# A fused attention and gated-MLP kernel: query weights built in wide pieces, early loads on two queues, a shorter inverse root, new load times

## The chip, the core and the metric

The kernel runs on one core of one Trainium2 chip. The core has a matrix engine (TensorE, in the profile PE, with its weight loads as PEld), a vector engine (VectorE, DVE), a scalar engine (ScalarE, ACT), GpSimd (POOL) and a sync engine (SyncE, SP) that issues DMAs; ACT and POOL can issue DMAs too. The metric is the device time of one execution in microseconds (us), and lower is better.

## The reference

All inputs are float32. Batch 8, 8 heads, 576 tokens, head size 64, 128 features.

```python
def phi(x):
    proj = np.einsum('bhsd,df->bhsf', x, w_phi)
    proj = proj - np.max(np.abs(proj), axis=-1, keepdims=True)
    return np.concatenate([np.exp(proj), np.exp(-proj)], axis=-1)
q_p, k_p = (phi(q), phi(k))
kv = np.einsum('bhsf,bhsd->bhfd', k_p, v)
z = np.sum(k_p, axis=2)
x = einsum(q_p, kv) / (einsum(q_p, z) + 1e-6)      # then heads side by side: (8, 576, 512)

h = np.maximum(x @ w_in, 0.0)                      # 512 -> 1024
u, v = h[..., :512], h[..., 512:]
v_n = (v - mean(v)) / np.sqrt(var(v) + 1e-06)
v_s = np.einsum('ts,bsd->btd', w_spatial, v_n) + b_spatial[None, :, None]
out = (u * v_s) @ w_out
```

## The kernel before

**Tiles.** The 576 tokens of a batch are 512 main tokens (four blocks of 128) and a tail of 64; the tails of two batches share one tile of 128 rows. The attention is worked in *units*, in a list written out at L567: a unit is a pair of heads of one batch (`pj` 0 to 3) over the main tokens, or the tail of a group of two batches. The list is: batch 0 pairs 0 and 1 (units 0, 1), the tail of group 0 (unit 2), pairs 2 and 3 (units 3, 4), batch 1 (units 5 to 8), the tail of group 1 (unit 9), batch 2 (units 10 to 13), batch 3, and so on to batch 7.

**A unit's path.** k and q are loaded as bfloat16 (`load`, L97, on POOL's DMA queue) and transposed: for batches 0 and 1 and for tails by PE through the identity (`a_transpose`, L249), for batches from 2 on by DMA transposes that SP issues three steps ahead (`cross`, L116, into `kT_b` and `qT_b`). `a_keys` (L271) multiplies by w_phi, takes the maxima on DVE (`mk`, L279) and the two exponentials on ACT (`kf`, L282). `a_scale` (L299) makes `em` on ACT (L302) and then multiplies v with it on POOL (`vs`, L307; for tails `tail_scale`, L317, into `vst`). `a_queries` takes the query maxima (`mq`, L293) and POOL splits them into two bfloat16 parts (`mhl`, L296 and L297); `a_max_t` (L326) transposes them on PE, and `a_qfeat` (L336) subtracts them within the matmul. From batch 2 on this uses the *query weights with maxima*, `wm`: eight blocks of 128 columns, the even ones holding the first half of w_phi with 16 rows of `sel` put below, the odd ones the second half with `sel` added (`weights_with_max`, L239). `q_even` (L245) copies a part of `qT_b` by DMA into `qt`. `a_kv` (L369), `a_num` and `a_x_t` follow, some steps later.

**The MLP.** When a batch's attention is done, `b_tasks` (L592) puts its MLP work into a queue, and `fill` (L620) hands out tasks from that queue between the attention's parts, by credit. Per batch: `b_v` (matmul on PE at L448, Relu on ACT at L450, statistics on DVE at L451 and L452), `b_root` (the inverse root of the variance on POOL, `root`, L454), `b_ln` (normalization on POOL, `normalize`, L464, one instruction of 128x512 per block, L465), `b_u` (L503), `b_s` (the spatial matmul, L524, which reads the normalized tiles `vn`) and `b_o` (L549). The spatial weights are loaded for batch 0 as `wsp`, `wspr` and `wspt` and transposed on PE into `w_spT` (`transpose_spatial`, L210); the bias goes into one row of `w_spT` for each of the two tails by four ACT copies at the end of that function. `vnt` holds the normalized tails; its other rows are filled once with a column of the identity so that the bias row counts.

**What sets the order.** The main loop (L713) runs `step(i)` for each unit and then the DMA work that the table `io` holds for that step. `pin` keeps an instruction in the order of the program on its engine. Each engine and each DMA queue runs its instructions in order, so on POOL a DMA issue stands in line with the scalings, and on SP a transpose that waits for a load holds up what is queued behind it. The start (L123 to L190) loads w_phi on ACT; k and q of heads 0 to 3, the k and q tails (into a staging tile `tails`), v and the v tail on SP in this order. DVE casts heads 0 and 1, POOL heads 2 and 3 and the tails. The other half of the heads is loaded by POOL in quarters (L185 to L190).

In the table of step numbers before the change, batch 2's k and q loads are issued at steps 4, 4, 6 and 7, the spatial weights at 4 and 5, the second part of w_in at 6, w_out at 8.

Of the kernel before, what the change touches and what calls it, by code (L numbers as in the profile page):

```python
# [16 lines left out]
def kernel(  # L17
# [105 lines left out]
    wphi_f = cpool.tile([P, F], FP32)  # L123
    for i in range(2):
        nc.scalar.dma_start(out=wphi_f[i * D:(i + 1) * D, :], in_=w_phi)
    alloc(0)
    first = {}
    for h0 in (0, 2):
        for x, t in (("k", k), ("q", q)):
            first[x, h0] = s2.tile([P, 2, NB * D], FP32, tag="ob", name="first", bufs=6)  # L130
            pin(nc.sync.dma_start)(out=first[x, h0], in_=main_ap(t, 0, h0, 2))
    alloc_tail(0)
    tails = ld.tile([P, H * NB, D], FP32, tag="v_f", name="tails")
    for n, t in enumerate((k, q)):
        for i in range(2):
            pin(nc.sync.dma_start)(out=tails[i * TL:(i + 1) * TL, n * H:(n + 1) * H, :], in_=tail_ap(t, i))
    load_v(0, 0)
    load_tail("v", 0)
    load_v(0, 1)
    ident = cpool.tile([P, P], BF16)  # L140
    make_identity(nc, ident)
    zero = cpool.tile([P, 1], BF16)
    pin(nc.vector.memset)(zero, 0.0)
# [25 lines left out]
    pin(nc.vector.memset)(vst[1], 0.0)  # L169
# [7 lines left out]
    pin(nc.scalar.copy)(out=vst[0].rearrange("p b s h d -> p (b s h d)"), in_=zero.to_broadcast([P, 4 * H * DA]))  # L177
# [3 lines left out]
    for i in range(2):  # L181
        fill_vnt(i, nc.gpsimd.tensor_copy)
    for x in ("k", "q"):
        pin(nc.gpsimd.tensor_copy)(out=half_tile(x, 0, 0)[:, 2:4], in_=first[x, 2])
    load("k", 0, 1, 0, 2)  # L185
    load("q", 0, 1, 0, 2)
    for n, x in enumerate(("k", "q")):
        pin(nc.gpsimd.tensor_copy)(out=gs[0][x], in_=tails[:, n * H:(n + 1) * H, :])
    load("k", 0, 1, 2, 2)
# [4 lines left out]
    wsp = s2.tile([P, NB, T0], BF16, tag="vn", name="wsp", bufs=2)  # L194
    wspr = cpool.tile([P, NB, TL], BF16)
    wspt = s2.tile([TL, S], BF16, tag="ob", name="wspt", bufs=6)
    bsp_row = s2.tile([P, S], FP32, tag="xT", name="bsp_row", bufs=3)
    nc.sync.dma_start(out=bsp_row[TL:TL + 1, :], in_=moe_b_spatial)
    nc.sync.dma_start(out=bsp_row[0:1, :], in_=moe_b_spatial)
# [10 lines left out]
    def transpose_spatial(i):  # L210

        pt = psum.tile([P, S], BF16, tag="bank", name="pt")
        if i < NB:
            sc = POS[i]
            for tp, c in enumerate(POS):
                nc.tensor.transpose(out=pt[:, tp * P:(tp + 1) * P], in_=wsp[:, c, bass.ds(sc, P, step=NB)],
                                    identity=ident)
            nc.tensor.transpose(out=pt[:, T0:S], in_=wspt[:, bass.ds(sc, P, step=NB)],
                                identity=ident[:TL, :TL])
            nc.vector.tensor_copy(out=w_spT[:, i, :], in_=pt)  # L220
            return
        for bl in range(2):
            lo = bl * TL
            for tp, c in enumerate(POS):
                nc.tensor.transpose(out=pt[lo:lo + TL, tp * P:(tp + 1) * P], in_=wspr[:, c, :], identity=ident)
            nc.tensor.transpose(out=pt[lo:lo + TL, T0:S], in_=wspt[:, T0:S], identity=ident[:TL, :TL])
            nc.vector.tensor_copy(out=w_spT[lo:lo + TL, NB + bl, :], in_=pt[lo:lo + TL, :])
        for bl, row in ((0, TL), (1, 0)):
            r = slice(row, row + 1)
            pin(nc.scalar.copy)(  # L230
                out=w_spT[r, NB + bl, 0:T0].rearrange("o (a b p) -> o a b p", a=2, b=2),
                in_=bsp_row[r, 0:T0].rearrange("o (p b a) -> o a b p", a=2, b=2))
            pin(nc.scalar.copy)(out=w_spT[r, NB + bl, T0:S], in_=bsp_row[r, T0:S])
# [4 lines left out]

    def weights_with_max(n):  # L239
        for j in range(4 * n, 4 * n + 4, 2):  # L240
            pin(nc.gpsimd.tensor_copy)(out=wm[:, j, :], in_=wphi2[:, 0:F])
            pin(nc.gpsimd.tensor_tensor)(out=wm[:, j + 1, :], in0=wphi2[:, F:2 * F], in1=sel[:, j + 1, :], op=ALU.add)
            pin(nc.gpsimd.tensor_copy)(out=wm[D:D + 2 * H, j, :], in_=sel[0:2 * H, j, :])
# [210 lines left out]
    def root(mv, r, n):  # L454

        var = small.tile([P, NB, 1], FP32, tag="var", name="var")
        rs = small.tile([P, NB, 2], FP32, tag="rs", name="rs")
        nc.gpsimd.tensor_scalar(out=var[r, 0:n], in0=mv[r, 0:n, 1:2], scalar1=1e-6, scalar2=None, op0=ALU.add)
        nc.gpsimd.tensor_tensor(out=rs[r, 0:n, 0:1], in0=var[r, 0:n], in1=neghalf[r, 0:n].unsqueeze(2), op=ALU.pow)
        nc.gpsimd.tensor_tensor(out=var[r, 0:n], in0=mv[r, 0:n, 0:1], in1=rs[r, 0:n, 0:1], op=ALU.mult)  # L460
        nc.gpsimd.tensor_scalar(out=rs[r, 0:n, 1:2], in0=var[r, 0:n], scalar1=-1.0, scalar2=None, op0=ALU.mult)
        return rs

    def normalize(dst, src, rs):  # L464
        nc.gpsimd.tensor_scalar(out=dst, in0=src, scalar1=rs[:, 0:1], scalar2=rs[:, 1:2],  # L465
                                op0=ALU.mult, op1=ALU.add)

    def b_v(b, j):
        d = st[b]
        if j == 0:  # L470
            d["vn"] = s2.tile([P, NB, HALF], BF16, tag="vn", name="vn", bufs=2)
            d["mv"] = small.tile([P, NB, 2], FP32, tag="mv", name="mv")
            d["vr"] = {}
        d["vr"][j] = s2.tile([P, HALF], BF16, tag="vr", name="vr", bufs=5)
        stats = small.tile([P, 6], FP32, tag="stats", name="stats")
        v_mm(lambda kc: d["xT"][:, kc, j * P:(j + 1) * P], d["vr"][j], slice(0, P), stats, d["mv"][:, j, :])

    def b_root(b):
        st[b]["rs"] = root(st[b]["mv"], slice(0, P), NB)

    def b_ln(b, j):
        d = st[b]
        normalize(d["vn"][:, j, :], d["vr"][j], d["rs"][:, j, :])

    def b_v_tail(g, bls):
# [6 lines left out]
        rstd = root(mv, r, 1)  # L492
        for bl in bls:
            r = slice(bl * TL, (bl + 1) * TL)
            normalize(vnt[g % 2][r, bl, :], vr[r], rstd[r, 0, :])
# [96 lines left out]
    def b_tasks(b):  # L592
# [8 lines left out]
        ts.append((0.0, lambda: b_root(b)))  # L601
# [79 lines left out]
    at(1, load_v, 1)  # L681
    at(2, load, "k", 1, 0)
    at(2, load, "q", 1, 0)
    at(3, load, "k", 1, 1)
    at(3, load, "q", 1, 1)
    at(4, load_weight, w_in_bf[:, :, HALF:DFF], cols[:, :, HALF:DFF])
    at(4, load_weight, wspt, moe_w_spatial[T0:S, :])
    at(5, tail_scale, 0, 1)
    at(5, load_weight, wsp, rows[:, :, 0:T0])
    at(5, load_weight, wspr, rows[:, :, T0:S])  # L690
    at(6, load_weight, w_in_bf[:, :, 0:HALF], cols[:, :, 0:HALF])
    at(8, load_weight, w_out_bf, moe_w_out.rearrange("(kc p) f -> p kc f", p=P))
    for u in units:
        i = u["i"]
        if not u["pair"] and u["g"] > 0:
            early = 1 if u["g"] > 1 else 0
            at(i - AT - early, load_tail, "k", u["g"])
            for x in ("q", "v"):
                at(i - AT + 1 - early, load_tail, x, u["g"])
        if u["pair"] and u["b"] >= XB:  # L700
            if u["pj"] == 0:
                for n, (x, y) in enumerate((("k", 0), ("q", 0), ("k", 1), ("q", 1))):
                    at((4, 4, 6, 7)[n] if u["b"] == XB else i - AB + n, load, x, u["b"], y)
# [4 lines left out]
    at(6, weights_with_max, 0)  # L708
    at(7, weights_with_max, 1)
# [39 lines left out]
```

## Time and profile before

Eight runs, device time in us; one execution was profiled.

| what | value |
|---|---|
| median of 8 runs | 284.66 us |
| lowest, highest | 282.31, 286.45 us |
| the profiled execution | 285.06 us, of which the trace's span is 283.0 us |
| PE busy | 259.7 us (92%), 3042 matmuls |
| DVE busy | 231.2 us (82%) |
| ACT busy | 219.6 us (78%) |
| POOL busy | 200.5 us (71%) |
| DMA | 42.43 MB, mean 150 GB/s |

The page gives a digit for each of 40 equal slices of the span (7.1 us each), tenths of the slice in which the engine was busy. A table of stages gives the same in microseconds for stretches that one chooses. The chain of waits is followed back from the last instruction: at each step to what released it. The timeline lists instructions in order of time, and in brackets the idle time before one and what ended it. A busy PE is not a PE at its peak, since its ends are modelled.

### The profile page before, as it was taken

The numbers are of one execution on the slowest core, as the hardware profiler recorded it, in microseconds if no ns is written. First come the engines' busy times: TensorE is split into PE (matmuls) and PEld (weight loads), VectorE is DVE, ScalarE is ACT, GpSimd is POOL, SyncE is SP. The second block draws the span as 40 slices with busy tenths as digits, with TensorE's granted clock in tenths as the row PEclk, the third lists the DMA queues.
The fourth block names the chain that finished last, engine by engine and source line by source line (L and its number), as shares of the span: only waits on it lengthen the run. The fifth ranks groups of instructions, "written<-read, shape, count | busy, mean of one in ns | idle before, by whom it ended". The sixth has DMA issues, their size and how long they took to land.

```text
span 283.0 us, 8175 instructions
## 1 busy us (share of the span) xinstructions
PE 259.7 (92%) x3042; PEld 172.9 (61%) x3042; DVE 231.2 (82%) x576; ACT 219.6 (78%) x499; POOL 200.5 (71%) x362
## 2 busy tenths in 40 slices
PE   2777988987999999999999999999999999999993
PEld 1466865754766577666666775666666765654441
DVE  7969997875799988998889989997889897566341
ACT  5679996979399997899889987899789977723601
POOL 5997999999958886799949974889548832411710
PEclk9979999999799999999999999999999999999999
DMA  7998999999977999989989999999765301120305
GB/s 203 227 216 111 157 141 228 126 175 185 215 78 164 145 216 188 165 185 225 231 101 122 205 251 147 204 199 225 92 122 132 86 2 63 50 76 37 112 3 185
DMA packets 85148, 42.43 MB, mean 150 GB/s; under 512 B 52146, under 2 KB 80498, under 8 KB 85108
## 3 DMA queue, kind: packets, MB, share of 16 engines
q1 hardware_dynamic: 60020, 30.95, 55.1%
q0 software_dynamic: 24928, 10.89, 35.6%
q8 instruction: 24, 0.39, 0.6%
q14 instruction: 16, 0.13, 0.2%
q10 hardware_dynamic: 160, 0.07, 0.1%
HBM read 32.85 MB, written 9.44 MB: 149 GB/s over the span
## 4 chain that ended last, share of the span: by engine, by line
PE 63%; POOL 12%; ACT 9%; DVE 6%; DMA 4%; issue 3%; SPq 0%; POOLq 0%; ACTq 0%; DVEq 0%
PE ps L524 10%; PE pv L448 10%; PE po L549 9%; PE ps L267 7%; PE pu L503 6%; ACT kf L282 5%; PE pv L379 4%; PE pn L399 4%; PE pq L345 3%; PE ps L525 3%; DMA q_bf<-in_q_dram 2%; POOL vst L61 2%; POOL vs L307 2%; DVE stats L451 2%; DMA first<-in_q_dram 2%
## 5 line engine op out<-in xcount | busy, mean ns | idle before, releaser
L282 ACT ACTIVATE kf<-ps 128x512 bf16<-128x512 f32 x144 | 76.1, 634 | 9.9 <-DVE mk L279 9.5
L307 POOL TENSOR_TENSOR vs<-v_f,em 128x512 bf16<-128x512 f32 x64 | 65.5, 1044 | 18.9 <-ACT em L302 17.5
L366 ACT ACTIVATE qf<-pq 128x512 bf16<-128x512 f32 x128 | 66.6, 618 | 10.1 <-PE pq L345 8.5
L279 DVE TENSOR_REDUCE mk<-ps 128x4 f32<-128x512 f32 x72 | 47.6, 677 | 1.2 <-PE ps L267 0.5
L293 DVE TENSOR_REDUCE mq<-ps 128x4 f32<-128x512 f32 x62 | 39.8, 681 | 2.7 <-PE ps L267 1.4
L524 PE MATMUL ps<-w_spT,vn 128*128 128x512 bf16 x128 | 34.1, 382 | 2.7 <-POOL vn L465 2.7
L527 DVE TENSOR_TENSOR uT<-ps,uT 128x512 bf16<-128x512 f32 x32 | 22.0, 687 | 16.7 <-PE ps L525 16.7
L451 DVE BATCH_NORM_STATS2 stats<-vr 128x6 f32<-128x512 bf16 (+1 forms) x40 | 26.7, 684 | 7.3 <-ACT vr L450 6.9
L549 PE MATMUL po<-w_out_bf,uT 128*128 128x512 bf16 x128 | 32.3, 379 | 0.0
L503 PE MATMUL pu<-xT,w_in_bf 128*128 128x512 bf16 x128 | 32.1, 379 | 0.0
L448 PE MATMUL pv<-w_in_bf,xT 128*128 128x512 bf16 x128 | 31.5, 379 | 0.1
L450 ACT ACTIVATE vr<-pv 128x512 bf16<-128x512 f32 (+1 forms) x40 | 23.5, 614 | 7.6 <-PE pv L448 6.4
L379 PE MATMUL pv<-vs,kf 128*128 128x66 bf16 x512 | 24.3, 193 | 1.3 <-ACT kf L282 1.3
L390 DVE TENSOR_TENSOR x<-pn,rc 128x256 bf16<-128x256 f32 x64 | 24.9, 417 | 0.3
L465 POOL TENSOR_SCALAR vn<-vr,rs 128x512 bf16<-128x512 bf16 x32 | 24.3, 766 | 1.1
L399 PEld LDWEIGHTS <-qf 128*128 128x128 bf16 x512 | 20.5, 98 | 7.1 <-issue 1.4
L505 ACT ACTIVATE uT<-pu 128x512 bf16<-128x512 f32 x32 | 19.6, 638 | 4.9 <-PE pu L503 3.2
L379 PEld LDWEIGHTS <-kf 128*128 128x128 bf16 x512 | 21.8, 97 | 2.5 <-issue 1.5
L552 ACT COPY ob<-po 128x512 f32<-128x512 f32 x18 | 11.0, 612 | 14.9 <-PE po L549 8.4
L399 PE MATMUL pn<-kv,qf 128*128 128x66 bf16 x512 | 22.0, 195 | 0.3 <-ACT qf L366 0.3
L381 PE MATMUL pv<-vst,kf 128*128 128x66 bf16 x128 | 21.2, 191 | 0.0
L524 PEld LDWEIGHTS <-vn 128*128 128x128 bf16 x128 | 11.7, 98 | 13.7 <-POOL vn L465 4.4
(133 smaller groups left out, 572.5 us busy)
## 6 DMA issues: line engine op xcount, KB each, us to landing
out_dram<-ob SPq DMA_DIRECT2D x32, 256.0 KB, 2.9
v_f<-in_v_dram SPq DMA_DIRECT2D x14, 512.0 KB, 6.6
k_bf<-in_k_dram POOLq DMA_DIRECT2D x14, 256.0 KB, 6.3
q_bf<-in_q_dram POOLq DMA_DIRECT2D x14, 256.0 KB, 6.7
qt<-qT_b SPq DMA_DIRECT2D x24, 64.0 KB, 4.8
v_tl<-in_v_dram SPq DMA_DIRECT2D x8, 128.0 KB, 3.5
v_f<-in_v_dram SPq DMA_DIRECT2D x1, 1024.0 KB, 9.3
w_in_bf<-in_moe_w_in_dram POOLq DMA_DIRECT2D x2, 512.0 KB, 9.6
```

What stands on the lines that cost most here:

```text
L279: nc.vector.tensor_reduce(out=u["mk"][:, hs], in_=pk, axis=AX.X, op=ALU.max, apply_absolute_value=True)
L282: nc.scalar.activation(out=u["kf"][:, s, hs, :], in_=pk, func=AF.Exp, bias=0.0, scale=sc)
L293: nc.vector.tensor_reduce(out=mq[:, 4 * half:4 * half + 4], in_=pq, axis=AX.X, op=ALU.max, apply_absolute_value=True)
L307: nc.gpsimd.tensor_tensor(out=vs[:, s, :, 0:D], in0=st[u["b"]]["v"][:, pj * H:(pj + 1) * H, :], in1=em[:, s, :].unsqueeze(2).to_broadcast( ...
L366: nc.scalar.activation(out=qf[:, s], in_=pq, func=AF.Exp, bias=0.0, scale=sc)
L379: nc.tensor.matmul(out=pv[:, hh, s, :], lhsT=u["kf"][:, s, 4 * hh + c, :], rhs=u["vs"][:, s, 4 * hh + c, :], start=(c == 0), stop=False)
L399: nc.tensor.matmul(out=pn[:, pos, :], lhsT=u["qf"][hh][:, s, pos, :], rhs=d["kv"][:, 2 * u["pj"] + hh, s, :], start=(s == 0), stop=(s == 1))
L448: nc.tensor.matmul(out=pv[r], lhsT=lhs(kc), rhs=w_in_bf[:, kc, HALF:DFF], start=(kc == 0), stop=(kc == KC - 1))
L451: nc.vector.bn_stats(out=stats[r], in_=dst[r])
L503: nc.tensor.matmul(out=pu, lhsT=w_in_bf[:, kc, dc * P:(dc + 1) * P], rhs=d["xT"][:, kc, :], start=(kc == 0), stop=(kc == KC - 1))
L524: nc.tensor.matmul(out=ps, lhsT=d["vn"][:, sp, cs], rhs=w_spT[:, sp, 0:T0], start=(sp == 0), stop=False)
L549: nc.tensor.matmul(out=po[r], lhsT=lhs(dc), rhs=w_out_bf[:, dc, :], start=(dc == 0), stop=(dc == KC - 1))
```

## The change

In words, part by part:

- **Start.** w_phi is issued first, on ACT; after it ACT also issues q of heads 2 and 3 and the q tails. SP issues k and q of heads 0 and 1, k of heads 2 and 3, the k tails, then the first half of v and the v tail. The tails are staged in the second half of batch 0's v tile instead of a tile of their own, so the second half of v is loaded after POOL has cast them. POOL casts k of heads 2 and 3, issues a quarter of k, casts q, issues a quarter of q.
- **Bias.** The bias rows are loaded by POOL right at the start, and POOL copies them into `w_spT` there; the four ACT copies at the end of `transpose_spatial` go.
- **Fills.** `vst[0]` is cleared by POOL as float32 words instead of an ACT copy of zeros; `vst[1]` by DVE as before. `vnt[1]` is filled at step 11 instead of at the start.
- **Query weights.** The even blocks of `wm` are written by two wide ACT copies at the start, the odd ones by one wide POOL addition at step 3, instead of twelve narrow POOL instructions at steps 6 and 7.
- **Spatial weights.** `wspr` goes; `wsp` holds all 576 columns and is loaded by one DMA at step 4. `wspt` moves to step 6.
- **Load times.** The second part of w_in moves from step 6 to 5, w_out from 8 to 9, batch 2's k and q from 4, 4, 6, 7 to 7, 7, 8, 9, its v to 8 and 9, batch 3's k and q by one step. The tail loads of group 1 are at steps 5 and 6.
- **Root.** The addition of the epsilon and the negated mean are made by DVE right after the statistics (`moments`), so the root on POOL is two instructions instead of four. For tails the root and the normalization become tasks of their own, behind the v matmuls.
- **Normalization.** For the last batch it runs on DVE.

```diff
+    tails = st[0]["v"][:, 2 * H:4 * H, :]
+    def load_first(x, h0, eng):
+        first[x, h0] = s2.tile([P, 2, NB * D], FP32, tag="ob", name="first", bufs=6)
+        pin(eng.dma_start)(out=first[x, h0], in_=main_ap(k if x == "k" else q, 0, h0, 2))
-        nc.scalar.dma_start(out=wphi_f[i * D:(i + 1) * D, :], in_=w_phi)
-    for h0 in (0, 2):
-        for x, t in (("k", k), ("q", q)):
-            first[x, h0] = s2.tile([P, 2, NB * D], FP32, tag="ob", name="first", bufs=6)
-            pin(nc.sync.dma_start)(out=first[x, h0], in_=main_ap(t, 0, h0, 2))
-    tails = ld.tile([P, H * NB, D], FP32, tag="v_f", name="tails")
-    for n, t in enumerate((k, q)):
+        pin(nc.scalar.dma_start)(out=wphi_f[i * D:(i + 1) * D, :], in_=w_phi)
+    load_first("k", 0, nc.sync)
+    load_first("q", 0, nc.sync)
+    load_first("q", 2, nc.scalar)
+    load_first("k", 2, nc.sync)
+    for n, t, eng in ((1, q, nc.scalar), (0, k, nc.sync)):
         for i in range(2):
-            pin(nc.sync.dma_start)(out=tails[i * TL:(i + 1) * TL, n * H:(n + 1) * H, :], in_=tail_ap(t, i))
+            pin(eng.dma_start)(out=tails[i * TL:(i + 1) * TL, n * H:(n + 1) * H, :], in_=tail_ap(t, i))
     load_v(0, 0)
     load_tail("v", 0)
-    load_v(0, 1)
...
-    pin(nc.vector.memset)(vst[1], 0.0)
+    bsp_row = s2.tile([P, S], FP32, tag="xT", name="bsp_row", bufs=3)
+    for r in (TL, 0):
+        pin(nc.gpsimd.dma_start)(out=bsp_row[r:r + 1, :], in_=moe_b_spatial)
+    for i, eng in ((0, nc.gpsimd), (1, nc.vector)):
+        pin(eng.memset)(vst[i].rearrange("p b s h d -> p (b s h d)").bitcast(FP32), 0.0)
...
-    pin(nc.scalar.copy)(out=vst[0].rearrange("p b s h d -> p (b s h d)"), in_=zero.to_broadcast([P, 4 * H * DA]))
-    for i in range(2):
-        fill_vnt(i, nc.gpsimd.tensor_copy)
+    fill_vnt(0, nc.gpsimd.tensor_copy)
+    for bl, r in ((0, TL), (1, 0)):
+        row, bias = w_spT[r:r + 1, NB + bl, :], bsp_row[r:r + 1, :]
+        pin(nc.gpsimd.tensor_copy)(out=row[:, 0:T0].rearrange("o (a b p) -> o a b p", a=2, b=2),
+                                   in_=bias[:, 0:T0].rearrange("o (p b a) -> o a b p", a=2, b=2))
+        pin(nc.gpsimd.tensor_copy)(out=row[:, T0:S], in_=bias[:, T0:S])
+    def alternate(t, i):
+        return t.rearrange("p (j two) f -> p j two f", two=2)[:, :, i, :]
+    pin(nc.scalar.copy)(out=alternate(wm, 0), in_=wphi2[:, 0:F].unsqueeze(1).to_broadcast([P, NP, F]))
+    pin(nc.scalar.copy)(out=alternate(wm[D:D + 2 * H], 0), in_=alternate(sel[0:2 * H], 0))
+    def odd_weights():
+        pin(nc.gpsimd.tensor_tensor)(out=alternate(wm, 1), in0=alternate(sel, 1),
+                                     in1=wphi2[:, F:2 * F].unsqueeze(1).to_broadcast([P, NP, F]), op=ALU.add)
     for x in ("k", "q"):
         pin(nc.gpsimd.tensor_copy)(out=half_tile(x, 0, 0)[:, 2:4], in_=first[x, 2])
-    load("k", 0, 1, 0, 2)
-    load("q", 0, 1, 0, 2)
+        load(x, 0, 1, 0, 2)
     for n, x in enumerate(("k", "q")):
         pin(nc.gpsimd.tensor_copy)(out=gs[0][x], in_=tails[:, n * H:(n + 1) * H, :])
+    load_v(0, 1)
...
-        nc.gpsimd.tensor_scalar(out=var[r, 0:n], in0=mv[r, 0:n, 1:2], scalar1=1e-6, scalar2=None, op0=ALU.add)
-        nc.gpsimd.tensor_tensor(out=rs[r, 0:n, 0:1], in0=var[r, 0:n], in1=neghalf[r, 0:n].unsqueeze(2), op=ALU.pow)
-        nc.gpsimd.tensor_tensor(out=var[r, 0:n], in0=mv[r, 0:n, 0:1], in1=rs[r, 0:n, 0:1], op=ALU.mult)
-        nc.gpsimd.tensor_scalar(out=rs[r, 0:n, 1:2], in0=var[r, 0:n], scalar1=-1.0, scalar2=None, op0=ALU.mult)
+    def moments(mv, r, n):
+        m = small.tile([P, NB, 2], FP32, tag="var", name="var")
+        nc.vector.tensor_scalar(out=m[r, 0:n, 0:1], in0=mv[r, 0:n, 1:2], scalar1=1e-6, scalar2=None, op0=ALU.add)
+        nc.vector.tensor_scalar(out=m[r, 0:n, 1:2], in0=mv[r, 0:n, 0:1], scalar1=-1.0, scalar2=None, op0=ALU.mult)
+        return m
+    def root(m, r, n):
+        nc.gpsimd.tensor_tensor(out=rs[r, 0:n, 0:1], in0=m[r, 0:n, 0:1], in1=neghalf[r, 0:n].unsqueeze(2), op=ALU.pow)
+        nc.gpsimd.tensor_tensor(out=rs[r, 0:n, 1:2], in0=m[r, 0:n, 1:2], in1=rs[r, 0:n, 0:1], op=ALU.mult)
+    def normalize(b, dst, src, rs):
+        eng = nc.vector if b == B - 1 else nc.gpsimd
+        eng.tensor_scalar(out=dst, in0=src, scalar1=rs[:, 0:1], scalar2=rs[:, 1:2], op0=ALU.mult, op1=ALU.add)
...
+    at(11, fill_vnt, 1, nc.gpsimd.tensor_copy)
+    at(3, odd_weights)
-    at(4, load_weight, wspt, moe_w_spatial[T0:S, :])
+    at(4, load_weight, wsp, rows)
-    at(5, load_weight, wsp, rows[:, :, 0:T0])
-    at(5, load_weight, wspr, rows[:, :, T0:S])
-    at(6, load_weight, w_in_bf[:, :, 0:HALF], cols[:, :, 0:HALF])
-    at(8, load_weight, w_out_bf, moe_w_out.rearrange("(kc p) f -> p kc f", p=P))
+    at(5, load_weight, w_in_bf[:, :, 0:HALF], cols[:, :, 0:HALF])
+    at(5, load_tail, "k", 1)
+    at(6, load_tail, "v", 1)
+    at(6, load_tail, "q", 1)
+    at(6, load_weight, wspt, moe_w_spatial[T0:S, :])
+    at(7, load, "k", 2, 0)
+    at(7, load, "q", 2, 0)
+    at(8, load, "k", 2, 1)
+    at(8, load_v, 2, 0)
+    at(9, load, "q", 2, 1)
+    at(9, load_v, 2, 1)
+    at(9, load_weight, w_out_bf, moe_w_out.rearrange("(kc p) f -> p kc f", p=P))
-                    at((4, 4, 6, 7)[n] if u["b"] == XB else i - AB + n, load, x, u["b"], y)
+                    at(i - AB + n + (u["b"] == 3), load, x, u["b"], y)
-    at(6, weights_with_max, 0)
-    at(7, weights_with_max, 1)
```

## The prediction

> **What bounds the kernel now.** I read the busy shares in slices first, then a table of 10 us stages, then the chain of waits where TensorE (PE) is not full, then single waits, last the landing times of the DMAs. From the slices:
>
> ```profile
> PE   2777988987999999999999999999999999999993
> DVE  7969997875799988998889989997889897566341
> POOL 5997999999958886799949974889548832411710
> ```
>
> PE falls short in the first ten slices (7.1 us each) and at the end. The stages give sizes (stretch, length, busy us of PE, PEld, DVE, ACT, POOL, then clock, DMA share, GB/s):
>
> ```profile
> 10.00:20.00 10.00, 6.66 (x57) 4.78 (x58) 7.61 (x22) 6.57 (x16) 9.98 (x16) 0.83 1.05 242
> 20.00:30.00 10.00, 8.22 (x159) 7.39 (x155) 10.00 (x29) 9.40 (x23) 7.97 (x12) 1.00 0.85 108
> ...
> 50.00:60.00 10.00, 8.87 (x109) 6.51 (x105) 7.80 (x22) 9.91 (x21) 9.17 (x21) 1.00 1.44 149
> 60.00:70.00 10.00, 8.38 (x103) 5.57 (x101) 6.85 (x15) 8.55 (x22) 9.30 (x17) 1.00 1.36 175
> ```
>
> PE idles 283.0 - 259.7 = 23.3 us: 8.9 before 20 (5.1 of it before its first transpose), 2.6 in 20 to 40, 4.8 in 40 to 80, 1.7 in 80 to 260, 5.2 after that (4.5 of it from 270 on, the drain of the last outputs). The edit leaves PE's instructions and their order as they are, so what can be won is idle time. From 19.4 to 42 VectorE (DVE) is full, so nothing on GpSimd (POOL) is worth anything there. The chain of waits, in pieces (start, us, what):
>
> ```profile
> 9.45 6.92 DMA q_bf<-in_q_dram
> ...
> 35.52 2.25 POOL vst L61 x3
> 37.77 0.68 POOL wsp L61
> 38.46 0.73 POOL wspr L61
> 39.19 1.39 POOL q_tl L61 x2
> ```
>
> A query load ends the wait at 16.4. From 29.4 to 43.3, and again from 54.0 to 70.7, the chain is POOL without a break: scalings, DMA issues, roots. The single waits (timeline, in brackets the idle time before the instruction) show where PE pays:
>
> ```profile
> 43.29 0.23 PE L328 MATMUL pt<-ident,mhl 128*128 128x128 bf16 x1 [1.56 <-POOL mhl L297]
> ...
> 59.07 0.38 PE L267 MATMUL ps<-wphi,kT_b 128*128 128x256 bf16 x2 [1.13 <-ACT qf L366]
> ...
> 69.22 0.39 PE L524 MATMUL ps<-w_spT,vn 128*128 128x512 bf16 x1 [1.25 <-POOL vn L465]
> 69.97 0.39 PE L524 MATMUL ps<-w_spT,vn 128*128 128x512 bf16 x1 [0.36 <-POOL vn L465]
> 70.72 0.61 PE L524 MATMUL ps<-w_spT,vn 128*128 128x512 bf16 x1 [0.36 <-POOL vn L465]
> ```
>
> The transfers are uneven. These are medians from issue to landing, the first for 18 to 34 us, the other two for 36 to 60:
>
> ```profile
> k_bf<-in_k_dram POOLq DMA_DIRECT2D x3, 256.0 KB, 4.3
> ...
> k_bf<-in_k_dram POOLq DMA_DIRECT2D x2, 256.0 KB, 12.7
> ...
> kT_b<-k_bf SPq DMA_TRANSPOSE x3, 11.0
> ```
>
> **What the Trainium skill says.** "DMA: Bandwidth & Descriptors", section "Issuing engines are not separate DMA queues": a second issuing engine saves only issue time, the 16 DMA engines are shared. The slow landings above, with transposes in flight, agree. So "two queues" is worth issue time, no bandwidth. Its section "SWDGE vs HWDGE vs iDMA": a load that casts must be issued by GpSimd; k, q and the weights do cast, so their issues (0.7 to 0.8 us each) stay on POOL. "GPSIMD Engine Reference", section 3.1: about 1.8 cycles an element for one input (768 ns for 512) and 2.6 for two; the trace has 767 ns (L465) and 1044 ns (L307). "VectorE: DVE Perf Modes", section "The perf-mode tier table": `tensor_scalar` from bf16 in SBUF runs four elements a cycle; no row of before has that form.
>
> **The change part by part.**
>
> *Start.* k and q of heads 0 and 1 keep their place on SP; q of heads 2 and 3 and the query tails go behind w_phi on ScalarE (ACT). ACT issues three more DMAs (0.5 + 2 x 0.7) before its table load, but loses the 1.95 us fill of vst: its w_phi casts end near 1.9 + 1.9 + 1.3 + 0.6 = 5.7, as before (5.71). POOL gains two bias issues (nearest rows 0.56 to 0.8 each), a 1056-word fill (DVE's took 0.94) and four bias copies (ACT's took 2.52 together; a POOL cast of 512 elements 0.61, so 1.6 to 3.2), and loses two of four vnt copies (1.37). It reaches its first k cast at 1.36 + 1.3 + 0.95 + 1.37 + 1.6 to 3.2 = 6.6 to 8.2, against 6.84 when the data came. The q load of the next half follows a k cast, a k issue and a q cast (0.6 + 0.8 + 0.6): issue at 8.9 to 10.3, against 9.45. In return the second half of v waits for the tails staged in it (POOL's q_tl cast, near 11 instead of an issue at 8.88), and batch 1's v queues behind it. Without that 0.5 MB and with no bias rows on SP, the load should land nearer 4.8 than 6.9 us after issue: near 14.8 instead of 16.4. DVE's idle around it (0.86 + 1.32 + 0.21 = 2.4 us) is the most to win; 2.3 us of PE work stands between the landing and DVE's mT copy, which leaves about 1.3. Late bias rows could make it -1.0. I take **-1.3** (range -2.4 to +1.0).
>
> *POOL from 28.6 to 56.2.* It is busy 25.0 of the 27.6 us up to the end of unit 8's scaling, counted instruction by instruction. Twelve wm pieces (4 x 0.30 + 4 x 0.43 + 4 x 0.28 = 4.0) become one two-input row of 512 elements (1.05, at step 3, behind unit 3's scaling) and two ACT copies at the start. One spatial issue goes (0.74); one q load of batch 2 and w_out (1.6) move behind the first normalization. I count 18.9 us in the new order, 6 us less. It buys only what PE idles. (a) Unit 6's maxima reach PE by 38, so the waits at 43.29 and 44.40 (1.56 + 0.17) go: **-1.4**, since DVE, full until 42, is next. (b) The bias copies leave ACT at 55.5 (2.52 us ahead of the qf that PE waited on at 59.07): **-0.9** of 1.13. (c) The root is two POOL instructions shorter (0.24 + 0.25, twice), and with the 6 us the normalized tiles come near 63, before PE asks: **-1.6** of 1.97. If ACT or DVE, 99% and 78% busy at 50 to 60, end these waits instead, (a) to (c) fall to about -1.5 together.
>
> *Loads of batch 2.* Both loads of its first half are issued from POOL near 42 and 45 instead of 31.3 and 32.0; SP's transposes, queued in order, wait for them. PE wants the first kT near 57.6 - 2.6 = 55. At 4.3 us for a load in a window now free of transposes and 5.3 for a transpose (its median at 56 to 92) it lands at 51.6; qT near 55.5 with 57 wanted. Margins of 2 to 3 us, so a small charge: **+0.7**, range 0 to +10 (the rows of 36 to 60).
>
> *Roots on DVE.* 16 roots x 2 small instructions. Not shown on DVE: nearest rows 0.06 (a memset of 5 elements) and 0.17 (L452), so 1.9 to 5.4 us of work. DVE is 82% busy and PE full from 80 on; only the tight stretches (90 to 110, 210 to 220) pass some on: **+0.8** (range 0 to +2.5).
>
> *End.* PE waits 0.36 + 0.36 on POOL's normalization at 269.0 and 269.75. On DVE each would take 0.2 us (an estimate from 693 ns on the VectorE page named above for 2048 elements), 0.69 at one element a cycle (L527): at 0.69 nothing is won, since an output copy now stands between the third and fourth. The pow at 1.04 stays. **-0.7** (range -0.7 to 0). The vnt fill moved to step 11 (1.4 us, POOL idles 2.6 at 79.8) is priced at nothing; without that cover unit 10's scaling comes 1.4 late.
>
> Sum: -1.3 - 1.4 - 0.9 - 1.6 - 0.7 + 0.7 + 0.8 = **-4.4 us**. Profiled: 285.06 - 4.4 = 280.7; it stood 0.4 above the median of 284.66, so the median should be **280.3**.
>
> **Rivals.**
> 1. *Hidden relief*: POOL's 6 us only bare DVE and ACT, and late bias rows eat the start. For: DVE is full from 19.4 to 42, ACT 99% at 50 to 60. Against: DVE idles 9.5 us of 40 to 72 (22.51 busy of 32). Middle parts -1.5, start and end -0.9, costs +0.8: 283.1.
> 2. *Late batch 2* (the slower side): place, PE's first kT_b matmul, 57.56 before. It decides once load plus transpose exceed 13 us (42 to 55); beyond 13 + 5.1 = 18.1 (5.1 being the sum without this charge) the whole gain is gone. With the landings of 36 to 60 they are 23.7, a loss of 10.7; with 8 + 12 = 20 the loss is 7, so 284.7 - 5.1 + 7 = 286.6. For: the transposes did take 11 us there. Against: they met 2 MB of casting loads and 1 MB of v; here the weights are issued by 35.
> 3. *All waits go*: start -2.4, (a) to (c) -4.7, end -0.7, no costs: 276.9.
>
> **How the numbers follow.** Forecast 0.56 (278.4 to 282.4), hidden relief 0.23, late batch 2 0.15 (286 to 290), all waits 0.06. About 0.5% (1.4 us) is what a measurement here tells from no change. Faster (below 283.2): 0.56 + 0.06 + half of 0.23 = 0.74; same: the other half plus a little of the third, 0.14; slower 0.12. The range, 277.8 to 285.0, leaves out most of the late case and part of the last.
>
> **What would show it.** q_bf's first load landing before 15.5, DVE's third mk (19.37) near 18; no wait on mhl near 42, no bias copies on ACT near 55, vn never waited for near 65; kT_b without a DMA wait; DVE's vn rows near 0.2 us. It is wrong if PE shows idle time before its first kT_b or qT_b matmuls, if POOL's first cast starts after 8.2, or if PE's idle time in 80 to 260 grows past 4 us.

## The result, and the profile after

After: 288.02 us, median of 21 runs (285.67 to 290.35). Before, in the same series: 284.56 us, median of 58 (281.81 to 287.18). Ratio 1.0126, 95% interval 1.0104 to 1.0148: slower by about 3.6 us, where 4.4 us less were forecast. The profiled execution of after took 285.94 us (span 284.2), 2.1 below its median, while that of before stood 0.4 above its own. Set side by side, the two traces therefore show less than the loss. I take places and waits from them and sizes from the ratios. One point below is 1% of the time of before, 2.8 us. A median given here covers all runs of a kernel, a ratio only its fast ones (within 1.5% of its fastest run) against those of before in the same series, so the two can differ by a few tenths of a point. The granted clock isn't what makes after slower: it averaged 0.990 in the runs of after and 0.987 in those of before.

The slices of after, from the page; each digit is a fortieth of the span:

```profile
PE   1778999999799889999999889999999999999993
DVE  7889999888599889999789989997889997665751
POOL 8999999899287884779866954798446842320200
```

TensorE (PE) is fuller from 43 to 70 than before, and has new gaps at the eleventh slice (70 to 78), near 90 to 110 and near 160. The table of stages (stretch, length, busy us of PE, PEld, DVE, ACT, POOL, then clock, DMA share, GB/s) gives the sizes:

```profile
10.00:20.00 10.00, 7.63 (x63) 5.42 (x63) 9.59 (x26) 6.77 (x19) 9.96 (x15) 1.00 1.19 247
...
40.00:50.00 10.00, 9.82 (x124) 6.94 (x121) 9.17 (x31) 9.08 (x23) 9.75 (x17) 1.00 1.17 130
50.00:60.00 10.00, 9.64 (x109) 6.71 (x108) 8.55 (x23) 6.84 (x16) 8.81 (x16) 1.00 1.23 188
60.00:70.00 10.00, 9.80 (x142) 7.25 (x141) 9.00 (x24) 8.40 (x22) 9.89 (x16) 1.00 1.11 145
70.00:80.00 10.00, 8.06 (x95) 5.22 (x93) 6.40 (x15) 6.58 (x15) 4.70 (x10) 1.00 1.33 220
...
100.00:110.00 10.00, 8.82 (x131) 6.36 (x130) 8.85 (x19) 7.75 (x19) 6.25 (x12) 1.00 1.33 236
...
160.00:170.00 10.00, 8.13 (x109) 5.80 (x108) 9.10 (x19) 7.88 (x19) 7.32 (x13) 1.00 1.31 202
...
260.00:270.00 10.00, 10.00 (x58) 4.70 (x58) 7.13 (x20) 5.51 (x10) 1.95 (x4) 1.00 0.21 79
```

The same stretches of before, as far as the prediction doesn't show them:

```profile
70.00:80.00 10.00, 9.64 (x113) 6.69 (x114) 7.25 (x18) 4.96 (x13) 7.36 (x14) 0.83 1.25 189
100.00:110.00 10.00, 9.58 (x125) 6.68 (x123) 8.12 (x20) 8.44 (x20) 8.32 (x15) 1.00 1.49 190
160.00:170.00 10.00, 10.00 (x147) 7.15 (x146) 9.02 (x21) 8.85 (x22) 8.18 (x14) 1.00 1.36 225
260.00:270.00 10.00, 9.28 (x57) 4.30 (x56) 4.56 (x11) 4.98 (x9) 6.74 (x13) 1.00 0.22 79
```

PE's busy time against before: 40 to 70 gains 3.7 us (29.26 against 25.52), 70 to 80 loses 1.6 (9.64 before), 100 to 110 loses 0.8 (9.58), 160 to 170 loses 1.9 (10.00), and 260 to 270 gains 0.7 (10.00 against 9.28). The same in the start times of the units' scaling exponentials (em): level with before within 0.3 us at units 3 to 7, ahead by 1.2 at unit 8 and 2.1 at unit 12, 0.7 at unit 16, level at unit 24, behind by 1.6 at unit 25 and 2.1 at unit 35. So the relief of the middle came, though part of the lead at unit 12 is the clock of 0.83 that the trace of before has in 70 to 80. The lead was spent between 77 and 111 and again near 164.

Single waits of PE in after, from the timeline (in brackets the idle time and what ended it):

```profile
20.57 0.19 PE L386 MATMUL pv<-vst,kf 128*128 128x66 bf16 x1 [1.37 <-POOL vst L61]
...
74.73 0.30 PE L384 MATMUL pv<-vs,kf 128*128 128x66 bf16 x4 [1.05 <-DVE qT_b L336]
...
103.08 0.41 PE L404 MATMUL pn<-kv,qf 128*128 128x66 bf16 x8 [1.18 <-DVE mq L298]
...
164.47 0.67 PE L432 MATMUL pn<-kv,qf_t 128*64 128x66 bf16 x16 [1.87 <-DVE mq L298]
```

None of these is a wait of before. The ones of before at 43.29, 59.07 and 69 to 71 are gone. The chain of waits in 60 to 80 has one piece that stands out:

```profile
66.65 7.52 DMA qt<-qT_b
...
74.26 0.41 DVE qT_b L336
74.67 0.68 DVE mk L284
```

### The profile page after: what moved, and what is told of

It is laid out like the page before. It is cut to its first block, busy times and chain, and to the rows that moved or that the text cites. A ratio compares the mean times of both kernels' runs of the same rounds, so it can differ in the third digit from the quotient of the medians.

```text
span 284.2 us, 8179 instructions
## 1 busy us (share of the span) xinstructions
PE 258.7 (91%) x3042; PEld 172.0 (61%) x3042; DVE 240.2 (85%) x612; ACT 216.1 (76%) x496; POOL 190.1 (67%) x320
## 4 chain that ended last, share of the span: by engine, by line
PE 65%; DVE 13%; ACT 10%; POOL 5%; DMA 3%; issue 2%; ACTq 0%; POOLq 0%; DVEq 0%
PE pv L453 10%; PE po L567 9%; PE ps L542 9%; PE pu L521 8%; PE ps L272 6%; ACT kf L287 6%; PE pv L384 4%; PE pn L404 4%; DVE mk L284 3%; PE pq L350 3%; ACT qf L371 3%; DMA qt<-qT_b 3%; DVE stats L456 2%; PE ps L543 2%; PE pn L432 2%
## 5 line engine op out<-in xcount | busy, mean ns | idle before, releaser
L467 POOL TENSOR_TENSOR rs<-var,neghalf 64x1 f32<-64x1 f32 (+1 forms) x16 | 12.7, 796 | 32.1 <-DVE var L462 32.0
L542 PE MATMUL ps<-w_spT,vn 128*128 128x512 bf16 x128 | 32.9, 379 | 0.0
L473 POOL TENSOR_SCALAR vn<-vr,rs 128x512 bf16<-128x512 bf16 x28 | 21.2, 767 | 1.0
```

What stands on the lines that cost most here:

```text
L542: nc.tensor.matmul(out=ps, lhsT=d["vn"][:, sp, cs], rhs=w_spT[:, sp, 0:T0], start=(sp == 0), stop=False)
```

## The first reading: what stands behind the new waits

*Near 74.* For units from batch 2 on, a transfer copies the queries' even rows from qT_b to qt (q_even), and VectorE (DVE) then writes the query maxima into other rows of qT_b (L336). The write waits until that transfer has landed (74.17, the write starts at 74.26). SP issues the transfer behind a transpose that waits for batch 2's last q load. With batch 2's loads late, that load lands at 64.18 (61.15 before), and the transfer is issued at 66.65 (63.17 before) and takes 7.5 us (7.05 before). In before it had landed at 70.22 and DVE came to the write at 76.44. In after DVE is ready at 71.05, by what the change gained up to there, and stands 3.21 us at L336. PE waits 1.05 us for that write and 0.40 for the key exponentials, which follow mk behind it.

*Near 100 and 160.* The 24 copies qt<-qT_b (L337, the second copy of the maxima, SBUF to SBUF) take 0.3 us in the median, but one took 2.05 us and one 2.32. DVE and POOL around the second, two timelines of after:

```profile
160.78 2.32 DVE L337 COPY qt<-qT_b 16x512 bf16<-16x512 bf16 x1
163.13 0.69 DVE L284 TENSOR_REDUCE mk<-ps 128x4 f32<-128x512 f32 x1
163.74 1.28 DVE L298 TENSOR_REDUCE mq<-ps 128x4 f32<-128x512 f32 x2
```

```profile
160.62 2.04 POOL L312 TENSOR_TENSOR vs<-v_f,em 128x512 bf16<-128x512 f32 x2
162.62 0.20 POOL L314 CAST vs<-em 128x32 bf16<-128x32 f32 x1
162.77 0.18 POOL L301 CAST mhl<-mq 128x8 bf16<-128x8 f32 x1
```

The copy starts 0.16 us after the first of GpSimd's (POOL's) two scalings and ends as they and two small casts are done. I call such a copy *held*. The Trainium skill, "SBUF — State Buffer", section "Who interferes with whom", states that copy, cast and `tensor_scalar` can run in a mode of VectorE that takes the port pair it shares with GpSimd, and that "Whoever issues first gets the shared pair for the whole instruction; the other **fully blocks** (not throttle)." The trace agrees for this copy: the scaling came first. The first copy of the maxima (L336), equal in shape but read from PSUM, never took more than 0.41 us.

This left three theories: R, the root's 32 small DVE instructions burden DVE by their own time; L, the late loads cost it; S, the start costs it. Later came H: the root costs because it moves copies under GpSimd's instructions, where they are held.

## Experiments: undo each part

**e1, the old root.** After, with GpSimd computing all four root instructions:

```diff
-            d["var"] = moments(d["mv"], slice(0, P), NB)
-        d["ln"] = vr, moments(mv, r, 1)
+        d["ln"] = vr, mv
     (root: the four GpSimd instructions of before, on mv)
```

> The kernel after, with the old root: GpSimd again computes all four instructions of each root, VectorE loses the 32 small ones (6.2 us of its work in the trace of after); everything else stays. Theory R (the roots on VectorE delay its maxima and cost TensorE most of the 3.6 us): ratio to before near 1.003, about 285.3 us, and TensorE idles less than 4 us between 80 and 260. Theory L (the late loads of batches 2 and 3 cost it) or theory S (the start costs it): ratio stays at 1.010 to 1.014, about 287.5 to 288.5 us, and the waits on VectorE's mq near 103 and 164 remain.

Measured: 283.19 us, ratio 0.9983 (0.9958 to 1.0009). More than R asked for: without the new root the change isn't slower. The waits at 103 and 164 are gone, the one near 76 (1.24 on DVE qT_b) stays, and PE waits another 0.83 us at 73.56 for a transpose of the late loads to land.

**e2, the new root alone**, in before:

```diff
-        rstd = root(mv, r, 1)
+        rstd = root(moments(mv, r, 1), r, 1)
+            d["var"] = moments(d["mv"], slice(0, P), NB)
     (root: GpSimd's two instructions of after)
```

> The kernel before with the new root alone: two of its four instructions move to VectorE. Theory R: slower by most of the loss, ratio 1.008 to 1.013, about 287 to 288 us. My prediction's step 'roots on VectorE' said +0.8, less some relief of GpSimd, so ratio 1.000 to 1.003. Theories L and S: ratio within 0.998 to 1.003.

Measured: 287.70 us, ratio 1.0110 (1.0081 to 1.0139): R's range, far from the +0.8 us predicted. Its copies near 100 and 161 took 2.08 and 2.61 us, and PE waited 1.22 and 2.33 behind them.

**e3, the old load places:**

```diff
-    at(7, load, "k", 2, 0)   (and q; 8, 9 for the second halves)
+    at((4, 4, 6, 7)[n] ..., load, x, u["b"], y)   (weights, tails, batch 3: old steps too)
```

> The kernel after with the old places of the loads in the step table (weights, spatial weights, tails of batches 2 and 3, batches 2 and 3), spatial weights still one load, all else as after. Theory L: ratio near 1.003, about 285.5 us, VectorE no longer waits 3.2 us on a DMA at 74. Theory R or S: ratio stays at 1.010 to 1.014; the wait at 74 may go, but nothing is won by the end.

Measured: 284.86 us, ratio 0.9993 (0.9962 to 1.0023). L is right as well: PE is busy 10.00 of 70 to 80.

**e4, the old start:**

```diff
-    load_first("q", 2, nc.scalar)     (first loads, tails: all by SyncE again)
-    fill_vnt(0, nc.gpsimd.tensor_copy)     (and the bias copies behind it)
+    for i in range(2):
+        fill_vnt(i, nc.gpsimd.tensor_copy)
+            pin(nc.scalar.copy)(out=w_spT[r, NB + bl, T0:S], in_=bsp_row[r, T0:S])     (with the transposes)
```

> The kernel after with the start of before: first loads all by SyncE, own tile for the tails, bias rows by SyncE and copied by ScalarE with the spatial transposes, fills by ScalarE and VectorE, both tail tiles filled by GpSimd at the start. The wide weights, the loads of later batches and the roots stay as after. Theory S: ratio near 1.003, about 285.5 us. Theories R and L: ratio 1.009 to 1.015, since in the traces the start of after stood within 0.5 us of before by unit 5, and the bias copies return to ScalarE near 55.

Measured: 286.24 us, ratio 1.0080 (1.0055 to 1.0106): half a point, between the two expectations.

## Experiments: is it the held copy?

**e5, e6, e7: the copy from PSUM**, in after, in before with the new root, and in before:

```diff
-            nc.vector.tensor_copy(out=even, in_=odd)
+            nc.vector.tensor_copy(out=even, in_=pt[0:2 * H, :].unsqueeze(1).to_broadcast([2 * H, 4, P]))
```

> The kernel after with one operand changed: VectorE's second maxima copy (qt<-qT_b, L337) reads the transposed maxima in PSUM, as the first does, instead of the first copy's output in SBUF. Same values, same place in every queue. Theory H (in the trace of after this SBUF-to-SBUF copy took 2.05 us at 99.66 and 2.32 us at 160.78, each time as long as GpSimd's two scaling instructions ran beside it, 0.3 to 0.5 us elsewhere; the new root only shifts GpSimd into it): every copy takes about 0.4 us, TensorE's waits of 1.18 at 103 and 1.87 at 164 go, ratio 0.998 to 1.004. Rival R (the 32 small root instructions themselves are VectorE's burden, 6.2 us of work): ratio stays at 1.009 to 1.013.

> The kernel before with the new root (ratio 1.011 alone) and the second maxima copy from PSUM. Theory H: the loss of the root alone goes, ratio 0.996 to 1.002, no copy longer than 0.5 us. Rival R: ratio 1.007 to 1.011.

> The kernel before with the second maxima copy from PSUM and nothing else. In the trace of before one copy of 24 was held (1.57 us at 167.08) with TensorE never idle there. Theory H: ratio 0.997 to 1.001, since before hardly meets the hold. If the copy from PSUM is worth something in itself (a shorter instruction everywhere), the ratio is below 0.995, and e5 and e6 must be read against that.

Measured: e5 1.0075 (1.0039 to 1.0111), e6 1.0006 (0.9979 to 1.0034), e7 1.0071 (1.0043 to 1.0099). The groups of instructions show the form before and after the edit (after, then e5; busy us and mean ns of one, idle time):

```profile
L337 DVE COPY qt<-qT_b 16x512 bf16<-16x512 bf16 x24 | 11.6, 483 | 0.8
```

```profile
L337 DVE COPY qt<-pt 16x512 bf16<-16x512 bf16 x24 | 10.0, 415 | 0.4
```

From PSUM no copy of the 24 was held (longest 0.417 us), but the usual one got longer (0.29 to 0.42 us). The edit isn't free: alone it costs 0.7 points, where e7 was expected to show none, and its single trace (284.60 us) doesn't say where. So e6 is read against e7: with unheld copies the new root is not a loss (1.0006 against 1.0071), with copies that can be held it costs 1.1 points (e2). That speaks for H and against R. e5 falls between the two expectations, 0.5 points better than after although the copy itself costs.

**e9 and e10: GpSimd's pace and DVE's instructions apart.** e9 keeps DVE's 32 instructions and lets GpSimd do all four as well, e10 has GpSimd's two alone:

```diff
e9   +            moments(d["mv"], slice(0, P), NB)     (result unused; root on mv, four instructions)
e10  rs[0] = pow(mv[1], neghalf); rs[1] = mv[0] * rs[0]     (no moments on DVE)
```

> The kernel after, where VectorE still computes its 32 small root instructions (their result is not used) and GpSimd again computes all four of each root: VectorE has the new work, GpSimd the old pace. Theory H, in the form that GpSimd's earlier arrival shifts its scalings into VectorE's maxima copy: the two copies near 100 and 160 take 0.3 to 0.6 us, ratio 0.998 to 1.005. If VectorE's own new instructions do the shifting or are the burden themselves: ratio 1.009 to 1.015.

> The kernel after with the root as GpSimd's two instructions alone (pow and product straight from the mean and variance); VectorE's 32 instructions are gone. It leaves out the addition of 1e-6 and the sign of the mean, so its output differs. GpSimd has the new pace, VectorE the old work. Theory H through GpSimd's earlier arrival: held copies of about 2 us remain near 100 and 160, ratio 1.006 to 1.012. If VectorE's own instructions are the cause: ratio 0.996 to 1.002 and no held copy.

Measured: e9 290.24 us, 1.0200 (1.0159 to 1.0241); e10 283.27 us, 0.9966 (0.9943 to 0.9989). Both went against what I expected of H: I had thought that GpSimd's earlier arrival alone does it. DVE's added instructions cost 1.6 points (e10 to after) and 2.2 (e1 to e9). The held copies show a finer pattern. Copies over 1 us:

```
                GpSimd root   DVE's 32   near 100    near 160
e1              four          none       -           -
e10             two           none       2.04        -
e9              four          yes        -           3.02
after, e2, e15  two           yes        2.05-2.08   2.31-2.61
```

With GpSimd's shorter root the copy near 100 is held: in after, e2 and e15 it starts 0.13 to 0.17 us behind the first scaling, in e1 0.85 us ahead of it. (In e10 it starts at 98.57, at the end of a DMA issue and 0.11 us ahead of a normalization, and is held through the normalization and one scaling, so there the recorded starts don't follow the rule of who came first.) With DVE's instructions another copy is held, near 160. Here a tenth of a us decides: in e1 it starts 0.09 us ahead of a normalization and isn't held, in e9 0.04 us behind one and is. Timelines of e1, DVE, then POOL:

```profile
160.26 0.29 DVE L337 COPY qt<-qT_b 16x512 bf16<-16x512 bf16 x1
```

```profile
160.35 0.84 POOL L471 TENSOR_SCALAR vn<-vr,rs 128x512 bf16<-128x512 bf16 x1
```

The same of e9 (its second normalization starts at 162.43):

```profile
162.47 3.02 DVE L337 COPY qt<-qT_b 16x512 bf16<-16x512 bf16 x1
```

```profile
161.68 1.51 POOL L477 TENSOR_SCALAR vn<-vr,rs 128x512 bf16<-128x512 bf16 x2
163.15 0.18 POOL L301 CAST mhl<-mq 128x8 bf16<-128x8 f32 x1
163.31 2.04 POOL L312 TENSOR_TENSOR vs<-v_f,em 128x512 bf16<-128x512 f32 x2
165.30 0.26 POOL L314 CAST vs<-em 128x32 bf16<-128x32 f32 x1
```

The copy is held through the rest of a normalization, a cast and both scalings, and PE waits 2.52 us for mq behind it. The hold near 100 is mild for the end (e10 has it and is no slower than before; its lead of 0.3 points may be the clock, which averaged 0.997 in its runs and 0.986 in those of before, where 0.01 of clock goes with 1.3 us). Each kernel with the one near 160 stands 1.1 to 2.2 points above its partner without it (e2 and before, e9 and e1, after and e1). In this table that hold and DVE's 32 instructions always come together, so it can't tell H from R; e6 against e7 does, and the stages of e15 below.

## Experiments: the parts one by one

**e8: what is left without root, loads and start.** After with all three undone; of the change remain the wide query weights, the merged spatial load, the tail's root as a task of its own and the last batch's normalization on DVE.

> The kernel after with old root, old load places and old start together: of the change only the wide query weights, the merged spatial load, the tail's root and normalization as tasks of their own, and the last batch's normalization on VectorE are left. If what the three undone parts cost is separate (e1: 1.4 points of ratio, e3: 1.3, e4: 0.5), the ratio is 0.979 to 0.985, about 279 us. If they cost through one common cause, it is 0.992 to 0.998, about 282.5 us.

Measured: 278.67 us, ratio 0.9838 (0.9788 to 0.9888). It beats both kernels; the three undone parts cost separately. Its stages, columns as above:

```profile
40.00:50.00 10.00, 8.51 (x103) 5.95 (x101) 7.98 (x25) 7.88 (x20) 9.66 (x18) 1.00 1.21 230
70.00:80.00 10.00, 10.00 (x137) 7.21 (x136) 9.72 (x21) 8.73 (x19) 5.80 (x11) 1.00 1.12 155
...
100.00:110.00 10.00, 10.00 (x134) 7.00 (x131) 8.36 (x20) 8.25 (x20) 6.45 (x12) 1.00 1.18 186
...
160.00:170.00 10.00, 10.00 (x124) 6.74 (x122) 9.08 (x21) 7.89 (x19) 6.43 (x10) 1.00 1.36 206
```

The gaps at 70, 100 and 160 are closed. The one at 40 to 50 is open again, a wait of 1.32 us on mhl at 42.45, where the loads of batch 2 are back in GpSimd's queue ahead of it.

**e15: e8 and the new root** (the edit of e1 taken back).

> The kernel of e8 with the new root and nothing else of the undone parts. Theory H as it stands now (GpSimd's shorter root and VectorE's two extra instructions each move a maxima copy under GpSimd's scalings, one near 100, one near 160): two copies of 2 us or more, TensorE waits of 1 us or more behind mq after each, ratio 0.994 to 1.000. If the copies are not held in this kernel and the ratio is still above 0.992, the root's own instructions are the cost; if neither, 0.981 to 0.988.

Measured: 285.13 us, ratio 1.0002 (0.9975 to 1.0028): 1.6 points for the root alone. Two copies were held, 2.05 and 2.31 us, and PE waited 1.19 and 1.88 us for mq behind them. DVE, then POOL, near the second:

```profile
159.25 2.31 DVE L336 COPY qt<-qT_b 16x512 bf16<-16x512 bf16 x1
```

```profile
159.09 2.04 POOL L311 TENSOR_TENSOR vs<-v_f,em 128x512 bf16<-128x512 f32 x2
```

The stages with the two holds:

```profile
100.00:110.00 10.00, 8.71 (x128) 6.17 (x127) 8.84 (x22) 7.75 (x21) 5.10 (x13) 1.00 1.41 213
...
160.00:170.00 10.00, 7.91 (x99) 5.94 (x99) 7.61 (x17) 6.46 (x16) 5.78 (x12) 0.83 1.31 200
```

A stretch of 10 us without a wait reads 9.89 in this trace. Against that PE idles 1.2 us in 100 to 110 and 2.0 in 160 to 170, the two holds, where e8 idles nothing. In 80 to 100, 140 to 150 and 210 to 220 it idles 1.3 us more than e8. So of some 4.5 us about 3.2 lie where the copies are held and the rest where the small instructions merely stand in DVE's queue ahead of mk and mq (PE's wait near 95 went from 0.58 to 1.20 us).

**e13: e8 and batch 2's late loads; e14: e8 and the new start.**

```diff
e13  -  at((4, 4, 6, 7)[n] if u["b"] == XB else i - AB + n, load, x, u["b"], y)
e13  +  at((7, 7, 8, 9)[n] if u["b"] == XB else i - AB + n, load, x, u["b"], y)
e13  +  at(8 + y if u["b"] == XB else i - AB + 1 + 2 * y, load_v, u["b"], y)
e14     (the edit of e4 taken back)
```

> The kernel of e8 (ratio 0.984) with one thing taken over from the change again: batch 2's q, k and v loads at the late places (steps 7, 7, 8, 9; v at 8 and 9). Weights, spatial weights, tails and batch 3 keep the old places. If the loads of batch 2 alone carry what undoing all load places gave (1.3 points): TensorE idles 2 us or more between 70 and 80 behind VectorE's qT_b copy or a transpose's landing, ratio 0.994 to 1.000. If the weights' and tails' places or batch 3's later loads carry it: ratio 0.981 to 0.988.

> The kernel of e8 with the new start and nothing else of the undone parts. If the start costs by itself what e4 showed (0.5 points): ratio 0.987 to 0.992, GpSimd's first k cast near 8.8, TensorE waiting for vst near 20. My prediction's -1.3 us for the start: ratio 0.978 to 0.981. Between: no cost by itself.

Measured: e13 280.97 us, 0.9891 (0.9843 to 0.9938); e14 279.50 us, 0.9827 (0.9796 to 0.9857). In e13 DVE waits again for the tile that the late transfer reads:

```profile
75.32 0.41 DVE L335 COPY qT_b<-pt 16x512 bf16<-16x512 bf16 x1 [3.15 <-PE ps L538]
```

The view names PE here. But the tile's q_even transfer, issued at 69.38, landed at 75.23, 0.09 us ahead of this write, the same lag as in after (74.17 and 74.26), so I take it to be that one. PE also waits 0.34 us for a transpose to land at 73.61. In the trace the late loads win 1.2 us near 42 (no wait on mhl) and lose 3.2 by unit 12. The ratios say 0.5 points, with intervals that overlap; whether the weights' and batch 3's places carry the rest of e3's 1.3 points stays open. e14 shows no cost of the start by itself, within intervals of 0.3 (e14) and 0.5 points (e8) each way. Its trace is 1.6 us behind that of e8 at unit 3 and has 0.9 of it back by unit 10, where ScalarE (ACT) no longer copies the bias. The 1.6 can't be put to the start: e13 has e8's start and is 1.5 us behind at unit 3 as well, since a k load landed later.

**e11, e12: the bias copies on ACT behind steps 0 and 1**, in after and in e8:

```diff
+    at(0, spatial_bias, 0)
+    at(1, spatial_bias, 1)     (two of ScalarE's four copies each)
```

> The kernel after with the four bias copies (2.66 us on GpSimd before its first k cast) on ScalarE instead, two behind step 0 and two behind step 1. If the start of after costs because these copies hold up GpSimd's casts and loads: first k cast on GpSimd near 6.2 instead of 8.8, the wait of 1.37 on vst at 20.57 shrinks by over 0.8 us, ratio near 1.008 (e4: undoing the whole start gave 0.5 points). If the new order of the transfers costs: unchanged within 0.3 points of 1.0126.

> The kernel of e8 (wide weights, last normalization on VectorE; ratio 0.984) with ScalarE's four bias copies moved from the spatial transposes near 55 to step 0 (two) and step 1 (two). My prediction's part (b) says these 2.5 us stand ahead of the query features that TensorE waits on for 1.13 us near 58: then that wait is gone and the ratio is 0.980 to 0.982. If the early copies delay ScalarE's first exponentials by as much, or if another wait takes its place: 0.983 to 0.987.

Measured: e11 287.62 us, 1.0097 (1.0065 to 1.0130); e12 280.37 us, 0.9859 (0.9817 to 0.9902). In e11 the first k cast starts at 7.55 instead of 8.80 and PE meets vst 0.8 us earlier, but waits as long for it (1.52 us). The 0.3 points between e11 and after lie within the intervals. In e12 the wait at 58 is gone and 0.9 us won there, but at 67.97 PE waits 0.71 for a query transpose instead, and a k load lands later at the start (PE's wait 2.53 at 16.40). Part (b) of the prediction was a real wait, and the next one behind it took 0.7 of the 0.9 us back.

Put together, ratios to before by which of the three parts is in (e13 has only part of the loads and is left out):

```
none 0.984 (e8)       root 1.000 (e15)         start 0.983 (e14)    root+start 0.999 (e3)
root+loads 1.008 (e4)   loads+start 0.998 (e1)   all three 1.013 (after)
```

The root costs 1.6, 1.7 and 1.4 points in its three pairs, the loads 0.8, 1.6 and 1.3, the start -0.1, -0.1 and 0.5. Why the start costs half a point only where root and loads are both in stays open; the intervals of after and e4 just touch.

## Why the prediction was wrong

- *The step that failed: "Roots on DVE", +0.8 (0 to +2.5).* It measured 4.1 us (e1) to 4.7 (e15). The instructions' own work was sized nearly right, 5.3 us in e15 and 6.2 in after against 1.9 to 5.4. What failed is the step from that work to its price: it reckoned only with a longer queue on DVE, which the tight stretches pass on to PE. But where VectorE's small instructions and GpSimd's shorter root move a copy by tenths of a us against GpSimd's instructions, 0.3 us become 2 to 3. One hold lies in a stretch that the step called tight (90 to 110), the dearer one, near 160, in none. By the stages of e15 the holds make 3.2 of 4.5 us, the queue 1.3. The trace of before had the sign, a copy of 1.57 us, with PE covered; the mean of the group (404 ns) hid it. DVE, then POOL, of before:

```profile
167.08 1.57 DVE L332 COPY qt<-qT_b 16x512 bf16<-16x512 bf16 x1
```

```profile
166.45 2.05 POOL L307 TENSOR_TENSOR vs<-v_f,em 128x512 bf16<-128x512 f32 x2
```

- *"Loads of batch 2", +0.7 (0 to +10).* It measured 2.2 to 4.4 us for all load places, 1.5 for batch 2's alone (e13). The step followed the tile to its first matmul and found 2 to 3 us of margin. In after it held: the first kT_b landed at 54.13 and the first qT_b at 54.37, where PE wanted them at 56.84 and 58.90. For a later tile of the batch it was thinner: PE waited for a qT_b to land in e1 (0.83 us), e9 (1.28) and e13 (0.34), which have the same places for these loads. The next in line, q_even's transfer and the write that it holds back, was not followed.
- *Start, -1.3 (-2.4 to +1.0).* The third mk was early (18.61 for 19.37), but not near 18, and the q load landed at 15.95, not before 15.5. GpSimd's first k cast started at 8.80, over the 8.2 named as the sign of failure: the bias copies took 2.66 us, within their bounds, but the two vnt copies 2.48 instead of 1.37. ACT's w_phi casts ended at 6.70, not 5.7. PE then waited 1.37 us for vst. Worth nothing alone (e14), +1.3 us with the rest (e4).
- *Relief of GpSimd: (a) -1.4, (b) -0.9, (c) -1.6.* The waits went as said. But (a) was bought by moving the loads of batch 2 and was paid back near 74 (e8, e13), and (b) stands before another wait (e12). (c) holds in e8 with the wide weights alone.
- *End, -0.7.* Right: PE full in 260 to 270. The four normalizations took 0.41 us each, not the 0.2 estimated: against the 0.69 that the step took for one element a cycle this is 1.7 times as fast, so the four elements a cycle, which the prediction took from the Trainium skill ("VectorE: DVE Perf Modes", section "The perf-mode tier table"), don't show in this form, and the measurement decides. That no row of before had this form was a misreading: its start has a bf16 `tensor_scalar` of 1024 elements, at 1.06 us.
- *vnt fill, nothing.* No wait on it in the trace of after.
- The rivals: late batch 2 was the right kind of case, at 286.6, with the wrong place (PE's first kT_b matmul). The declared sign "PE's idle time in 80 to 260 over 4 us" came true: 6.4 us, from 1.7.

In sum the parts without root, loads and start gave -4.6 us (e8; -6.0 to -3.2 by its interval), where (c) and the end made -2.3: unit 11 stands 1.0 us ahead of before in the traces and unit 12 4.8, part of it because the trace of before has a clock of 0.83 in 70 to 80. So the gains were real, and larger than said without (a). The root and the loads cost some 3.5 and 2.5 us more than priced, and the start's gain didn't come. That the direction was wrong comes from the root and the loads together: with either one undone (e1, e3) the change is level with before.

## What to carry to other kernels

Before work is moved between VectorE and GpSimd, look at the longest instance of each SBUF-to-SBUF copy, cast or `tensor_scalar`, not at its mean: one that stretches over the GpSimd instructions beside it marks a place where the time can depend on which starts first. Follow a later load beyond its first reader, to the writes that wait until the tile has been read. And undo a bundle part by part: here the bundle lost 1.3% and held a part that wins 1.6%.

## What the runs showed of the hardware

- A held VectorE copy lasts through several GpSimd instructions in a row, not one: 2.32 us over two scalings and two casts, 3.02 us over part of a normalization, a cast and two scalings. The sentence quoted from the Trainium skill speaks of the one instruction; here the copy came in only after a run of them. In e10 it came in between two scalings, after a normalization and the first one (2.04 us). A copy that started together with a DMA issue of GpSimd took 0.51 to 0.52 us instead of 0.28 (at 100.77 in before, 100.45 in e1, 95.96 in e8).
- In all traces only forms of VectorE that read and write SBUF alone ever took over 1.5 times their shortest time: the maxima copy, a 128x4 `tensor_scalar` (0.15 us usual, up to 1.12), and at the start the 1024-element `tensor_scalar` (2.16 beside GpSimd's fills, 1.06 in before), a 128x512 cast (0.82 for 0.41) and a 128x8 `tensor_tensor` (0.54 beside GpSimd's vnt copies in before, 0.10 in after). `bn_stats`, which reads SBUF too, stayed within 0.65 to 0.70 us.
- The other way round as well: GpSimd's two vnt copies (128x512 bf16) at the start took 1.09 and 1.43 us beside that `tensor_scalar` and VectorE's casts. In before three of the four took 0.60 to 0.61 us and the last, beside the `tensor_scalar`, 1.07.
